# Linear attention and a mixture of experts in one kernel: VectorE's order in the middle of the attention

## The chip, the cores and the metric

One core of a Trainium2 chip runs the whole program. The metric is the time of one execution in microseconds on the device. TensorE does the matrix products (PE in the profile, PEld its weight loads), VectorE (DVE) and ScalarE (ACT) the elementwise work, GpSimd (POOL) a share of it and the indirect DMAs; SyncE (SP) issues the other DMAs.

## The reference, cut to what matters

```python
def phi(x):                                   # x: (8, 8, 576, 64) of q or k
    proj = einsum('bhsd,df->bhsf', x, w_phi)  # 128 features
    proj = proj - max(abs(proj), axis=-1)
    return concat([exp(proj), exp(-proj)])
kv  = einsum('bhsf,bhsd->bhfd', phi(k), v)
z   = sum(phi(k), axis=2)
num = einsum('bhsf,bhfd->bhsd', phi(q), kv)
den = einsum('bhsf,bhf->bhs', phi(q), z) + 1e-06
x   = num / den                               # as 4608 rows of 512
```

Then, over the 4608 rows: rows with `x @ w_skip > 0` go to the expert with the largest of 8 gate logits, `y = gate * (relu(x @ w1[e]) @ w2[e])`, and `x + y` is their output; the other rows stay as they are.

## The kernel before

The attention is cut into 16 units of k and 16 of q: a batch and four heads each, with `u.hq` 0 or 1 for the half of the heads. A unit has five items `i`: 0 is the tail of 64 tokens per head, 1 to 4 are blocks of 512 columns. The k stream runs six steps ahead of the q stream, and a step `t` does one stage of one item of each: transpose (`st_t`, lag 0), projection and subtraction of the largest magnitude (`st_proj`, lag 1), exponentials (`st_exp_k`, `st_exp_q`, lag 3; q is first transposed on TensorE), use (lag 4: `st_use_k` sums kv in bank K, `st_use_q` makes numerator, gate logits and denominator in a bank O), and for a finished k unit the sum z over partitions (`st_z`, lag 5) and the augmented matrix `kva` (`st_aug`, lag 6), which the numerators of that unit's q read.

PSUM has two buffers for projections (P), one for q's transposes (U), one for kv (K) and two for everything else (O): numerators, z sums, augmentation, ranks, indices and counts. Each use holds its buffer until the engine that reads it is done.

On VectorE a step has: transposes of raw blocks (`xT`, L331; tails `xTt`, L329), a reduce (`m`, L361) and a subtract (`u`, L364) over a projection of up to 1024 columns, and for each numerator a norm (`norm`, L467): add to the denominator (`den`, L471), reciprocal (`rec`, L475), two products (`xm` L482, `lgm` L483). When both halves of a batch are done, `post` picks each row's expert in a chain of small instructions (`L`, `mx`, `d`, `key`, `km`, `oh`, `OH`, then `ss`, `gt` and a reciprocal for the gate), and later `rank` (TensorE, then `rm`, `rki`, `rkp`, `RKH`, `st`, `Stot`, `rm4`; the one-hots `OP` are made on GpSimd), `index` (TensorE, then `acc4`) and `rest` (rows to the output) follow. Work that is put off stands in the list `later` with a due step; CFG["post"] is (4, 7, 7) for these three. For batch 5 (`EB`) the list also gets two `pick`s and `pick_third`, which choose the first experts' tokens so that their gathers can start early.

Order: `tc.manual_schedule` keeps the named engines in the order in which the program is written; engines that it does not name are ordered by the framework's planner at build time. Step 0 to 7 are one hand-written list (`RAMP`). From step 8 to 77 two steps are written as a pair, in the order of the list `PAIR`: `L` runs what is due, `T` transposes, `q` and `k` exponentials, `P` projections, `Z` and `A` z and augmentation, `U` use, `D` loads of v. TensorE and ScalarE are in program order up to step 78; SyncE and VectorE only up to step 17, and from 18 on they are ordered by the planner:

```python
man.enter_context(tc.manual_schedule(engines={PE, Activation}))     # closed at t == 79
ramp.enter_context(tc.manual_schedule(engines={SP, DVE}))           # closed at t == 18
PAIR = [('L', 0), ('T', 0), ('T', 1), ('q', 0), ('k', 0), ('P', 0), ('P', 1), ('Z', 0), ('L', 1),
        ('q', 1), ('A', 0), ('k', 1), ('U', 0), ('U', 1), ('D', 0), ('D', 1)]
```

After the attention the expert stage runs (the second half of the file); the change does not touch it. It needs the attention's memory, the picks and the first weights.

Of the kernel before, what the change touches and what calls it, by code (L numbers as in the profile page):

```python
# [24 lines left out]
def kernel(  # L25
# [230 lines left out]
    with actx:  # L256
# [77 lines left out]
        def st_proj():  # L334
# [11 lines left out]
            for u, i in todo:  # L346
# [11 lines left out]
                nj += m  # L358
            pv = p.rearrange("p h (j f) -> p j h f", f=NF)[:, 0:nj]
# [7 lines left out]
            for u, i, a, b in spans:  # L367
                u.u[i] = uu[:, a:b, :]

# [97 lines left out]
        def norm(o, xdst, ldst, shape):  # L467

            den = small.tile([P, 4], F32, tag="den", name="den")
            rec = small.tile([P, 4], F32, tag="rec", name="rec")  # L470
            nc.vector.tensor_scalar(  # L471
                out=den.rearrange("p (t o) -> p t o", o=1), in0=o[:, :, NA1:NAUG],
                scalar1=1e-6, scalar2=None, op0=ALU.add,
            )
            nc.vector.reciprocal(out=rec, in_=den)  # L475
            rv = rec.rearrange("p (t o) -> p t o", o=1)
            a, c = shape

            def sh(x):
                return x.rearrange("p (a c) d -> p a c d", a=a)  # L480

            nc.vector.tensor_tensor(out=xdst, in0=sh(o[:, :, 0:D]), in1=sh(rv.broadcast_to([P, 4, D])), op=ALU.mult)  # L482
            nc.vector.tensor_tensor(  # L483
                out=ldst, in0=sh(o[:, :, D:NA1]), in1=sh(rv.broadcast_to([P, 4, NA1 - D])), op=ALU.mult)

        def st_use_q(u, i):
# [5 lines left out]
            if i == 0:  # L492
# [11 lines left out]
                if u.hq == 0:  # L504
# [6 lines left out]
                     lgt[:, 0, u.hq * 4:(u.hq + 1) * 4, :].rearrange("p (a h) e -> p a h e", a=2), (2, 2))  # L511
# [13 lines left out]
            if u.hq == 0 and i == 1:  # L525
# [5 lines left out]
            norm(ov, xm[u.hq][:, 2 * th:2 * th + 2, 0:4 * D].rearrange(  # L531
                "p a (h r d) -> p a r h d", h=2, d=D)[:, :, pr],
                 lgm[:, 2 * th:2 * th + 2, h0:h0 + 2, :], (2, 2))
            if i == 4:
                c = slice(0, 4 * D)
                if u.hq == 0:
                    def store_half(b=u.b, xm=xm):
                        nc.sync.dma_start(out=rowm[b][:, :, c], in_=xm[0])
                        if b % 2 == 1:
                            nc.sync.dma_start(out=rowt[b // 2][:, c], in_=xt_of[b // 2][0][0][:, 0])  # L540
                    later.append((now[0] + 2, store_half))
                else:
                    post(u.b)

# [3 lines left out]
        def post(b):  # L548
# [25 lines left out]
            for xx, lg, o, n in reversed(parts):  # L574
                nc.vector.tensor_reduce(
                    out=L[:, o:o + n, :], in_=lg.rearrange("p t h e -> p t e h"), axis=AX.X, op=ALU.add,
                )
            nc.vector.tensor_reduce(out=mx[:, 0:nt], in_=L[:, 0:nt, 0:E], axis=AX.X, op=ALU.max)
            nc.vector.tensor_tensor(out=d[:, 0:nt], in0=L[:, 0:nt, 0:E], in1=bc(mx[:, 0:nt], nt, E), op=ALU.subtract)
            nc.vector.scalar_tensor_tensor(  # L580
                out=key[:, 0:nt], in0=d[:, 0:nt], scalar=0.0,
                in1=desc.rearrange("p (o e) -> p o e", o=1).broadcast_to([P, nt, E]),
                op0=ALU.is_equal, op1=ALU.mult,
            )
            nc.vector.tensor_reduce(out=km[:, 0:nt], in_=key[:, 0:nt], axis=AX.X, op=ALU.max)
            nc.vector.tensor_tensor(out=oh[:, 0:nt], in0=key[:, 0:nt], in1=bc(km[:, 0:nt], nt, E), op=ALU.is_equal)
            nc.vector.scalar_tensor_tensor(
                out=OH[:, T, :], in0=L[:, 0:nt, E:E + 1].broadcast_to([P, nt, E]), scalar=0.0, in1=oh[:, 0:nt],
                op0=ALU.is_gt, op1=ALU.mult,
            )  # L590

            def gate():
                nc.scalar.activation(out=ex[:, 0:nt], in_=d[:, 0:nt], func=AF.Exp)
                nc.vector.tensor_reduce(out=ss[:, 0:nt], in_=ex[:, 0:nt], axis=AX.X, op=ALU.add)
                nc.vector.tensor_scalar(out=gt[:, 0:nt], in0=ss[:, 0:nt], scalar1=1e-9, scalar2=None, op0=ALU.add)
                for xx, lg, o, n in parts:
                    nc.scalar.activation(
                        out=xx[:, :, 4 * D + 1:4 * D + 2], in_=sid[:, t0 + o:t0 + o + n].rearrange("p (t o) -> p t o", o=1), func=AF.Copy)
                    nc.vector.reciprocal(out=xx[:, :, 4 * D:4 * D + 1], in_=gt[:, o:o + n].rearrange("p (t o) -> p t o", o=1))

# [6 lines left out]
            if last:  # L607
                gate()
                store_rows()
            else:  # L610
                later.append((now[0] + 2, gate))
                later.append((now[0] + 4, store_rows))
# [4 lines left out]
            def rank():  # L617

# [13 lines left out]

                if last:
                    count()
                rm = sm("rm", [5, E])
                rki = sm("rki", [5], I32)
                rkp = sm("rkp", [5], I32)
                nc.vector.tensor_tensor(out=rm[:, 0:nt], in0=r.rearrange("p (t e) -> p t e", e=E), in1=OH[:, T, :], op=ALU.mult)
                with nc.allow_low_precision(reason="sums of integers below 2**24 written as integers"):
                    nc.vector.tensor_reduce(out=rki[:, 0:nt], in_=rm[:, 0:nt], axis=AX.X, op=ALU.add)  # L640
                nc.vector.tensor_scalar(out=rkp[:, 0:nt], in0=rki[:, 0:nt], scalar1=127, scalar2=None, op0=ALU.bitwise_and)
                for c in range(2):
                    for t in range(nt):
                        (nc.vector if last else nc.gpsimd).tensor_scalar(  # L644
                            out=OP[:, t0 + t, c, :], in0=iota_p, scalar1=rkp[:, t:t + 1],
                            scalar2=wcol[:, NT:NT + 1] if c else wcol[:, t0 + t:t0 + t + 1], op0=ALU.is_equal, op1=ALU.mult)
                nc.vector.tensor_scalar(out=RKH[:, T], in0=rki[:, 0:nt], scalar1=7, scalar2=None, op0=ALU.arith_shift_right)
                if not last:
                    count()
                if b > EB:  # L650
                    return
                for s in range(S):
                    nc.vector.scalar_tensor_tensor(
                        out=rm4[:, 0:nt, :, s], in0=bc(RKH[:, T], nt, E), scalar=float(s), in1=OH[:, T, :],
                        op0=ALU.is_equal, op1=ALU.mult,
                    )
# [121 lines left out]
        for t in range(n + OFF + LA):  # L778
            if t == 18:
                ramp.close()  # L780
# [537 lines left out]
```

## Time and profile before

| | us |
|---|---|
| median of 3 runs | 603.95 |
| lowest, highest | 603.88, 605.79 |
| profiled execution | 603.57 |
| its span, first to last instruction | 601.6 |

In the profile a row has a time or a total in microseconds, the line of the kernel (L361), the engine, the operation, and `out<-in` by the program's tile names. In brackets or behind `<-` stands what released an engine that had been idle. A matmul's end is modelled, a wait is counted from that end, and a weight load's wait is listed apart. Where rows of the timeline are merged, the count stands at the end (x64).

### The profile page before, as it was taken

The numbers are of one execution on the slowest core, as the hardware profiler recorded it, in microseconds if no ns is written. First come the engines' busy times: TensorE is split into PE (matmuls) and PEld (weight loads), VectorE is DVE, ScalarE is ACT, GpSimd is POOL, SyncE is SP. The second block draws the span as 40 slices with busy tenths as digits, with TensorE's granted clock in tenths as the row PEclk, the third lists the DMA queues.
The fourth block names the chain that finished last, engine by engine and source line by source line (L and its number), as shares of the span: only waits on it lengthen the run. The fifth ranks groups of instructions, "written<-read, shape, count | busy, mean of one in ns | idle before, by whom it ended". The sixth has DMA issues, their size and how long they took to land. (4 is left out here: it accounts for less than half of the span.)

```text
span 601.6 us, 18718 instructions
## 1 busy us (share of the span) xinstructions
PE 557.7 (93%) x7486; PEld 466.8 (78%) x7486; DVE 498.9 (83%) x1085; ACT 328.9 (55%) x649; POOL 375.6 (62%) x399
## 2 busy tenths in 40 slices
PE   5799899999999999999799799899999998999993
PEld 3577678778877778777667799798999887988892
DVE  5888998999989999899897759767789987867841
ACT  4466465666656655565444554354758666556720
POOL 6645486596675866848664645994668683638031
PEclk9999999999999999999899899899999999999998
DMA  8987998998668756531235297598787678777500
GB/s 146 160 143 141 181 184 177 208 186 194 139 147 194 150 135 155 122 95 46 87 115 177 75 325 260 156 310 286 216 275 241 231 269 299 255 225 255 191 20 30
DMA packets 250297, 108.33 MB, mean 180 GB/s; under 512 B 192481, under 2 KB 235617, under 8 KB 250208
## 3 DMA queue, kind: packets, MB, share of 16 engines
q1 hardware_dynamic: 244640, 97.45, 62.0%
q0 software_dynamic: 3200, 9.45, 4.3%
q8 instruction: 60, 0.98, 0.7%
q10 hardware_dynamic: 2368, 0.22, 0.3%
q14 instruction: 29, 0.24, 0.1%
HBM read 83.86 MB, written 24.02 MB: 179 GB/s over the span
## 5 line engine op out<-in xcount | busy, mean ns | idle before, releaser
L387 POOL TENSOR_TENSOR z<-ek 128x512 f32<-128x512 f32 x64 | 81.1, 1274 | 79.7 <-ACT ek L380 61.5
L200 POOL TENSOR_TENSOR w<-wraw_c,w 128x256 fp32r<-128x256 f32 x108 | 99.0, 950 | 48.3 <-ACT w L195 48.2
L195 ACT ACTIVATE w<-wraw_c 128x1024 fp32r<-128x1024 f32 x96 | 98.0, 1051 | 7.6 <-DMA wraw_c<-in_moe_w_dram 5.9
L200 DVE TENSOR_TENSOR w<-wraw_c,w 128x1024 fp32r<-128x1024 f32 x69 | 90.6, 1327 | 9.3 <-ACT w L195 7.8
L361 DVE TENSOR_REDUCE m<-ps_P 128x8 f32<-128x1024 f32 (+3 forms) x86 | 88.6, 1030 | 3.7 <-PE ps_P L354 3.7
L364 DVE TENSOR_TENSOR u<-ps_P,m 128x1024 f32<-128x1024 f32 (+3 forms) x86 | 88.7, 1032 | 3.1
L520 PEld LDWEIGHTS ps_O<-kva,eq 128*64 128x64 f32 x2048 | 74.4, 137 | 16.0 <-DVE cs L710 4.4
L354 PE MATMUL ps_P<-wsrc,xT 64*64 64x128 f32 x2048 | 74.5, 280 | 11.1 <-DVE xT L331 6.4
L406 ACT ACTIVATE eq<-ps_U 128x512 f32<-128x512 f32 x64 | 38.1, 596 | 83.1 <-PE ps_U L400 82.1
L520 PE MATMUL ps_O<-kva,eq 128*64 128x74 f32 x2048 | 77.3, 229 | 6.3 <-DVE cs L710 3.7
L354 PEld LDWEIGHTS ps_P<-wsrc,xT 64*64 64x64 f32 x2048 | 58.5, 136 | 22.8 <-issue 10.4
L422 PE MATMUL ps_K<-ek,v 128*64 128x256 f32 x512 | 68.4, 388 | 0.0
L903 POOL DMA_INDIRECT out_dram<-o,si x22 | 32.5, 1477 | 57.1 <-DVE si L902 50.6
L970 PE MATMUL ps_O<-w,hh 128*128 128x512 f32 x160 | 63.9, 399 | 0.7 <-DVE o L917 0.7
L644 POOL TENSOR_SCALAR OP<-iota_p,rkp,wcol 128x128 bf16<-128x128 f32 x62 | 48.5, 797 | 13.4 <-DVE rec L475 7.2
L400 PE MATMUL ps_U<-ident,u 128*128 128x128 f32 x288 | 49.2, 289 | 0.4 <-DVE den L471 0.3
L331 DVE STREAM_TRANSPOSE xT<-raw 128x512 f32<-128x512 f32 x64 | 43.5, 694 | 6.7 <-PE ps_P L354 3.4
L974 PE MATMUL ps_O<-w,hh 128*128 128x512 f32 x120 | 47.0, 391 | 0.1
L379 ACT ACTIVATE ek<-u 128x512 f32<-128x512 f32 x64 | 41.0, 640 | 11.1 <-DMA wgs<-in_moe_w_gate_dram 6.1
L975 PE MATMUL ps_O<-w,hlo 128*128 128x512 f32 x120 | 46.8, 390 | 0.0
L422 PEld LDWEIGHTS ps_K<-ek,v 128*64 128x64 f32 x512 | 32.9, 137 | 16.0 <-issue 6.2
L393 POOL TENSOR_TENSOR z<-z,ekt 64x512 f32<-64x512 f32 x32 | 40.8, 1274 | 5.1 <-DMA xg<-xrows,idg 2.8
(254 smaller groups left out, 1202.7 us busy)
## 6 DMA issues: line engine op xcount, KB each, us to landing
wraw_c<-in_moe_w_dram SPq DMA_DIRECT2D x96, 512.0 KB, 5.1
raw<-in_q_dram SPq DMA_DIRECT2D x64, 144.0 KB, 3.5
raw<-in_k_dram SPq DMA_DIRECT2D x60, 144.0 KB, 3.1
v<-in_v_dram SPq DMA_DIRECT2D x64, 128.0 KB, 2.6
out_dram<-xm SPq DMA_DIRECT2D x16, 512.0 KB
xrows<-xm SPq DMA_DIRECT2D x8, 516.0 KB, 3.9
xrows<-xm SPq DMA_DIRECT2D x8, 512.0 KB, 4.7
vt<-in_v_dram SPq DMA_DIRECT2D x32, 32.0 KB, 4.3
```

Source lines behind the costliest of these rows:

```text
L195: nc.scalar.activation(out=hi, in_=raw, func=AF.Copy)
L200: eng.tensor_tensor(out=lo[:, r], in0=raw[:, r], in1=hi[:, r].bitcast(F32), op=ALU.subtract)
L354: nc.tensor.matmul(p[s * 64:s * 64 + 64, hd, (nj + j) * NF:(nj + j + 1) * NF], xT[r, g * P + s * 64:g * P + s * 64 + 64], wsrc[r], start=T ...
L361: nc.vector.tensor_reduce(out=m.rearrange("p (j h) -> p j h", h=2), in_=pv, axis=AX.X, op=ALU.max, apply_absolute_value=True)
L364: nc.vector.tensor_tensor(out=uu[:, 0:2 * nj, :].rearrange("p (j h) f -> p j h f", h=2), in0=pv, in1=m.rearrange("p (j h o) -> p j h o", h ...
L387: zeng.tensor_tensor(out=z, in0=e[:, 0:2, :], in1=e[:, 2:4, :], op=ALU.add)
L400: nc.tensor.transpose(t[:, tt * P:(tt + 1) * P], uu[:, tt, :], ident)
L422: nc.tensor.matmul(o[hd * 64:hd * 64 + 64, :], u.v[:, 2 * hd + pr, g * D:(g + 1) * D], u.e[i][:, 2 * j + hd, :], start=(g == 0), stop=False,)
L520: nc.tensor.matmul(ov[s * 64:s * 64 + 64, 2 * j + hd, :], e[:, half, j, hd, s * 64:s * 64 + 64], kva[:, half, 2 * pr + hd, :], start=(half ...
L644: (nc.vector if last else nc.gpsimd).tensor_scalar(out=OP[:, t0 + t, c, :], in0=iota_p, scalar1=rkp[:, t:t + 1], scalar2=wcol[:, NT:NT + 1 ...
L970: nc.tensor.matmul(y[sub], hh[:, t], wh[:, fi, :], start=first, stop=False)
L974: nc.tensor.matmul(y[sub], hh[:, t], wl[:, fi, :], start=False, stop=False)
```

## The change

VectorE joins the engines in program order for steps 0 to 77, until t is 78; SyncE leaves program order at step 8 in place of 18. The order written out for VectorE is a new one. A pair now begins with the first transposes; then the norms of the pair before run together (`norms`: both additions, both reciprocals, then the products); then come the exponentials, both projections on TensorE, and only after them their reduces and subtracts (`st_diff`, `V`), the second transposes, both kv sums (`u`) and then both numerators (`n`). The chain of `post` becomes a generator; `hook` issues its next instruction, and stands after the norms, after each reduce and after each subtract, and inside a norm that has no partner. `drain` issues what is left of a batch's chain before its rank or index. The index comes 10 steps after `post` (8 for batch 5) in place of 7, the picks 9 and 11 in place of 8 and 10, the third at 13 in place of 12; what is due is looked at once in a pair.

```diff
-        PAIR = [('L', 0), ('T', 0), ('T', 1), ('q', 0), ('k', 0), ('P', 0), ('P', 1), ('Z', 0), ('L', 1), ('q', 1), ('A', 0), ('k', 1), ('U', 0), ('U', 1), ('D', 0), ('D', 1)]
+        PAIR = [('T', 0), ('N', 0), ('H', 0), ('q', 0), ('k', 0), ('P', 0), ('P', 1), ('L', 1), ('V', 0), ('V', 1), ('Z', 0), ('q', 1), ('A', 0), ('k', 1), ('T', 1), ('u', 0), ('u', 1), ('n', 0), ('n', 1), ('D', 0), ('D', 1)]
...
-        ramp.enter_context(tc.manual_schedule(engines={mybir.EngineType.SP, mybir.EngineType.DVE}))
+        dve = ExitStack()
+        dve.enter_context(tc.manual_schedule(engines={mybir.EngineType.DVE}))
+        ramp.enter_context(tc.manual_schedule(engines={mybir.EngineType.SP}))
...
-            if t == 18:
+            if t == 8:
                 ramp.close()
+                paired[0] = True
+            if t == 78:
+                drain()
+                norms()
+                drain()
+                paired[0] = False
+                dve.close()
...
+        def st_diff(got):
+            p, nj, spans = got
...
             nc.vector.tensor_reduce(
                 out=m.rearrange("p (j h) -> p j h", h=2), in_=pv, axis=AX.X, op=ALU.max, apply_absolute_value=True)
+            hook()
...
             for u, i, a, b in spans:
                 u.u[i] = uu[:, a:b, :]
+            hook()
...
+        def norms():
...
+            for o, xdst, ldst, den, rec in todo:
+                nc.vector.tensor_scalar(
+                    out=den.rearrange("p (t o) -> p t o", o=1), in0=o[:, :, NA1:NAUG],
+                    scalar1=1e-6, scalar2=None, op0=ALU.add,
+                )
+            if len(todo) == 1:
+                hook()
+            for o, xdst, ldst, den, rec in todo:
+                nc.vector.reciprocal(out=rec, in_=den)
+            if len(todo) == 1:
+                hook()
+            for o, xdst, ldst, den, rec in todo:
+                rv = rec.rearrange("p (t o) -> p t o", o=1)
+                nc.vector.tensor_tensor(
+                    out=xdst, in0=sh(o[:, :, 0:D]), in1=sh(rv.broadcast_to([P, 4, D])), op=ALU.mult)
+                nc.vector.tensor_tensor(
+                    out=ldst, in0=sh(o[:, :, D:NA1]), in1=sh(rv.broadcast_to([P, 4, NA1 - D])), op=ALU.mult)
...
+        def hook():
+            while chain:
+                try:
+                    next(chain[0][1])
+                    return
+                except StopIteration:
+                    chain.pop(0)
...
-                for n, f in zip(CFG["post"], (rank, index, rest)):
+                for n, f in ((4, rank), (8 if b == EB else 10, index), (7, rest)):
                     later.append((now[0] + n, f))
                 if b == EB:
                     for j in range(2):
-                        later.append((now[0] + CFG["post"][2] + 1 + 2 * j, lambda j=j: pick(j)))
-                    later.append((now[0] + CFG["post"][2] + 5, pick_third))
+                        later.append((now[0] + 9 + 2 * j, lambda j=j: pick(j)))
+                    later.append((now[0] + 13, pick_third))
```

Inside the chain the order is as before, with a `yield` after each instruction (after two of the four `rm4`, and after the exponential that the gate needs); the gate and the row store are its last pieces, where they used to be entries of `later` 2 and 4 steps on.

## Rows read from the trace of the kernel before

**Rows 1.** Page, part 1: busy time of each engine, its share, instructions

```profile
PE 557.7 (93%) x7486; PEld 466.8 (78%) x7486; DVE 498.9 (83%) x1085; ACT 328.9 (55%) x649; POOL 375.6 (62%) x399
```

**Rows 2.** Busy time in two stretches (us, times), clock, DMA share, GB/s

```profile
60.00:290.00 230.00, 219.08 (x4340) 176.36 (x4334) 219.00 (x532) 136.01 (x325) 160.45 (x148) 1.00 0.71 155
...
337.00:602.00 265.00, 246.94 (x1565) 221.84 (x1562) 193.66 (x336) 139.34 (x210) 153.30 (x168) 0.98 0.67 222
```

**Rows 3.** Waits of TensorE's matmuls, 60 to 290 us: total, times, longest

```profile
PE ps_O L499 <- ACT kva L461: 2.2, 3, 1.6
PE ps_P L354 <- DVE u L364: 2.1, 4, 1.0
PE ps_O L520 <- ACT kva L461: 2.0, 6, 0.3
PE ps_O L664 <- DVE den L471: 1.9, 3, 0.7
PE ps_O L664 <- POOL OP L644: 1.7, 3, 0.6
```

**Rows 4.** Waits of its weight loads there, those on another engine's work

```profile
PEld L664 <- POOL OP L644: 3.8, 9, 0.7
...
PEld ps_O L499 <- ACT kva L461: 3.5, 3, 2.0
PEld ps_O L520 <- ACT kva L461: 3.5, 6, 0.6
PEld ps_P L354 <- DVE u L364: 3.1, 4, 1.2
```

**Rows 5.** Waits of VectorE, 60 to 290 us

```profile
DVE xT L331 <- PE ps_P L354: 2.5, 7, 0.6
DVE den L471 <- PE ps_O L520: 2.1, 5, 0.4
DVE acc L670 <- PE ps_O L664: 0.9, 2, 0.5
```

**Rows 6.** Timeline of VectorE, 99 to 106 us: start, duration, instruction

```profile
99.53 1.19 DVE L361 TENSOR_REDUCE m<-ps_P 128x8 f32<-128x1024 f32 x1
100.82 1.22 DVE L364 TENSOR_TENSOR u<-ps_P,m 128x1024 f32<-128x1024 f32 x1
...
104.83 0.14 DVE L471 TENSOR_SCALAR den<-ps_O 128x4 f32<-128x4 f32 x1
105.00 0.18 DVE L475 RECIPROCAL rec<-den 128x4 f32<-128x4 f32 x1
105.22 0.42 DVE L482 TENSOR_TENSOR xm<-ps_O,rec 128x256 f32<-128x256 f32 x1
105.56 0.18 DVE L483 TENSOR_TENSOR lgm<-ps_O,rec 128x36 f32<-128x36 f32 x1
105.66 0.15 DVE L471 TENSOR_SCALAR den<-ps_O 128x4 f32<-128x4 f32 x1
```

**Rows 7.** Groups of VectorE, 60 to 290 us: busy, mean ns, idle before

```profile
L361 DVE TENSOR_REDUCE m<-ps_P 128x8 f32<-128x1024 f32 x36 | 43.3, 1203 | 0.0
...
L361 DVE TENSOR_REDUCE m<-ps_P 128x6 f32<-128x768 f32 x24 | 22.5, 936 | 0.0
...
L471 DVE TENSOR_SCALAR den<-ps_O 128x4 f32<-128x4 f32 x52 | 7.8, 149 | 2.1 <-PE ps_O L520 2.1
```

**Rows 8.** Timeline of all engines: two projections on TensorE, merged

```profile
136.06 1.98 PE L354 MATMUL ps_P<-wsrc,xT 64*64 64x128 f32 x64
```

**Rows 9.** Timeline of all engines about the first pick

```profile
292.58 1.98 PE L520 MATMUL ps_O<-kva,eq 128*64 128x74 f32 x32 [3.12 <-DVE cs L710]
...
293.44 1.21 POOL L213 DMA_INDIRECT xg<-xrows,idg  x1 [1.13 <-DVE idg L222]
...
298.69 1.27 POOL L393 TENSOR_TENSOR z<-z,ekt 64x512 f32<-64x512 f32 x1 [2.79 <-DMA xg<-xrows,idg]
```

**Rows 10.** Waits of VectorE, 24 to 60 us: the one on a load

```profile
DVE xTt L329 <- DMA raw<-in_q_dram: 1.7, 1, 1.7
```

More of the change, by code (lines that the diff above doesn't have):

```diff
@@ L465, in st_aug, with sh @@
             kva_of[u.g] = kva
[L467 to L484, printed above, removed]
+        def sh(x):
+            return x.rearrange("p (a c) d -> p a c d", a=2)
@@ new lines, in norms @@
+        def norms():
+            todo = []
+            for o, xdst, ldst, then in undone:
+                den = small.tile([P, 4], F32, tag="den", name="den")
+                rec = small.tile([P, 4], F32, tag="rec", name="rec")
+                todo.append((o, xdst, ldst, den, rec))
+            for o, xdst, ldst, den, rec in todo:
[15 more added lines that the diff above has]
+                    out=ldst, in0=sh(o[:, :, D:NA1]), in1=sh(rv.broadcast_to([P, 4, NA1 - D])), op=ALU.mult)
+            then = [d[3] for d in undone if d[3]]
+            undone.clear()
+            for f in then:
+                f()
@@ new lines, in norm, with drain @@
+        def norm(o, xdst, ldst, then=None):
+            undone.append((o, xdst, ldst, then))
+            if not paired[0]:
+                norms()
+        undone, chain, paired = [], [], [False]
+        def hook():
+            while chain:
+                try:
+                    next(chain[0][1])
+                    return
+                except StopIteration:
+                    chain.pop(0)
+        def drain(b=None):
+            while [c for c in chain if b in (None, c[0])]:
+                hook()
@@ L486, in st_use_q, with run_later @@
+        def run_later(b, g, front=False):
+            chain.insert(0 if front else len(chain), (b, g))
+            if not paired[0]:
+                drain()
         def st_use_q(u, i):
@@ L609, in post @@
                 store_rows()
-            else:
-                later.append((now[0] + 2, gate))
-                later.append((now[0] + 4, store_rows))
+            run_later(b, choose())
             S = 4
@@ L641, in rank @@
[L641 to L656, printed above, removed]
+                def turned():
+                    if last:
+                        count()
+                    rm = sm("rm", [5, E])
+                    rki = sm("rki", [5], I32)
+                    rkp = sm("rkp", [5], I32)
+                    nc.vector.tensor_tensor(
+                        out=rm[:, 0:nt], in0=r.rearrange("p (t e) -> p t e", e=E), in1=OH[:, T, :], op=ALU.mult)
+                    yield
+                    with nc.allow_low_precision(reason="sums of integers below 2**24 written as integers"):
+                        nc.vector.tensor_reduce(out=rki[:, 0:nt], in_=rm[:, 0:nt], axis=AX.X, op=ALU.add)
+                    yield
+                    nc.vector.tensor_scalar(out=rkp[:, 0:nt], in0=rki[:, 0:nt], scalar1=127, scalar2=None, op0=ALU.bitwise_and)
+                    for c in range(2):
+                        for t in range(nt):
+                            (nc.vector if last else nc.gpsimd).tensor_scalar(
+                                out=OP[:, t0 + t, c, :], in0=iota_p, scalar1=rkp[:, t:t + 1],
+                                scalar2=wcol[:, NT:NT + 1] if c else wcol[:, t0 + t:t0 + t + 1], op0=ALU.is_equal, op1=ALU.mult)
+                    yield
+                    nc.vector.tensor_scalar(
+                        out=RKH[:, T], in0=rki[:, 0:nt], scalar1=7, scalar2=None, op0=ALU.arith_shift_right)
+                    yield
+                    if not last:
+                        count()
+                        yield
+                    if b > EB:
+                        return
+                    for s in range(S):
+                        nc.vector.scalar_tensor_tensor(
+                            out=rm4[:, 0:nt, :, s], in0=bc(RKH[:, T], nt, E), scalar=float(s), in1=OH[:, T, :],
+                            op0=ALU.is_equal, op1=ALU.mult,
+                        )
+                        if s % 2 == 1:
+                            yield
@@ L660, in index @@
                     return
+                drain(b)
                 ix = bank("O")[:, 0:nsh]
@@ L790 @@
                 if c == "L":
+                    now[0] = t + (1 if first else 0)
                     for w, f in [x for x in later if x[0] <= now[0]]:
```

114 lines of the change are left out of this document (68 added, 46 removed).

## The prediction

> **What bounds the kernel now.** I read four views in this order. The busy times [rows 1] put TensorE at 93% of the span and VectorE at 83%. That is a mean over unlike stages, so the stretches come next [rows 2]: from 60 to 290 us, the middle of the attention, TensorE is busy 219.08 of 230 us and VectorE 219.00, both at 95%, with the clock at 1.00. From 337 us on the experts run and VectorE is at 73%. So the change lies in a stage where two engines look full at once, and the reader has to ask which of them waits for the other.
>
> The waits answer that. In 60 to 290 us TensorE's matmuls waited for other engines 9.9 us in 19 places (2.2, 2.1, 2.0, 1.9 and 1.7) [rows 3]; its weight loads waited for the same releasers 13.9 us in the four largest groups [rows 4]. VectorE in turn waited for TensorE only 5.5 us in its three largest groups [rows 5]. So neither has slack: TensorE follows its fixed order with few holes, and VectorE has hardly any idle time. But "busy" on VectorE hides something that the timeline shows [rows 6]. A reduce at 99.53 lasts 1.19, and the subtract that reads its result starts at 100.82, 0.10 after the reduce's end. The small product at 105.56 lasts 0.18, and the next norm's addition, which does not need it, starts at 105.66, 0.08 before that end. An instruction behind the one it reads costs about 0.18 us more than one that doesn't. One norm is a chain of such: addition at 104.83, reciprocal at 105.00, products at 105.22 and 105.56, next instruction at 105.66, so 0.83 us.
>
> **The bound in numbers, for ten steps.** The window holds 60 steps (36 + 24 reduces, [rows 7]), so ten steps take 230 / 6 = 38.3 us. TensorE without waits: by its matmuls 9.9 us could go, by its weight loads 13.9. I take 12.7, near the upper end: a matmul's end is modelled, and I estimate from the two views that it covers some 0.15 us of each of the 19 waits, so 9.9 + 2.8. That is 2.1 us of each ten steps (bounds 1.65 to 2.3), and TensorE alone needs 36.2. VectorE: 230 - 5.5 = 224.5 us of work with its bubbles, 37.4 per ten steps.
>
> **Part 1: two q norms interleaved.** Written as two additions, two reciprocals, then the products, no norm instruction stands behind the one that it reads. An independent small instruction starts 0.10 after the one before (105.56 to 105.66); the first two steps of a norm, 0.17 and 0.22, come down to 0.10 each, so 0.19 a norm and 0.38 for two: 1.28 us in place of 1.66 [rows 6]. There are 52 norms in the window [rows 7]; with the skipped tails 22 pairs of two and 8 singles, so 22 x 0.38 = 8.4 us, and some 0.8 for the singles, whose gaps take a chain instruction. The norms also move: they run at the head of the next pair, behind the first transposes. They hold an O bank that much longer, but the next user of one (rank or index, z) comes on TensorE only after both projections, 1.98 us for 64 matmuls [rows 8]. VectorE now waits there in order for the last numerator; queued behind it are the next reduces, which wait for projections that TensorE issues still later, so that wait costs little. The price if that cover is gone is the 1.28 us of the norms in each pair.
>
> **Part 2: chain instructions between the large ones.** About 20 of them in ten steps fill gaps behind a reduce or subtract. Their own time stays. Now the planner puts a transpose or a chain instruction into many of the reduce-subtract gaps; afterwards the transposes are elsewhere and some 3 or 4 of 10 such gaps stay open. No row gives the new count, so I bound it: 0 to 20 x 0.18 = 3.6 us of loss in the window, and take 1.5, below the middle, since some stand open now as at 99.53 [rows 6].
>
> VectorE afterwards: 224.5 - 8.4 - 0.8 + 1.5 = 216.8 us, or 36.1 per ten steps (35.9 without new gaps; 37.4 to 38.0 if interleaving brings nothing).
>
> **Part 3: kv sums ahead of numerators, index later.** On TensorE nothing is added. The numerators now stand behind both kv sums. Waits for `kva` (2.2 + 2.0, [rows 3]) end: ScalarE's copies have the kv sums' time to finish. The index matmuls come at +10 steps in place of +7, so the 1.7 us behind GpSimd's one-hots go, and, with the norms at the head of the pair, the 1.9 us for an O bank. The 2.1 us in which a projection waited for a subtract go if VectorE is not late: both subtracts of a pair stand ahead of its second transposes. VectorE may be late by about one projection (half of 1.98 us, [rows 8]) plus the q transposes before TensorE stalls, since the first projection of a pair needs only transposes of the pair before.
>
> **Part 4: the picks.** The choice of the first experts' tokens moves from steps 77 and 79 to 79 and 81. Today the first costs TensorE 3.12 us: its count matmul holds an O bank until VectorE's `cs`, and a numerator starts only at 292.58 [rows 9]. At 79 TensorE's order is the planner's again. I bound the gain by 3.1 and, with the work moved into the tail, -1, and take 1.5.
>
> **Queues.** SP's order is free from step 8 rather than 18: no row shows what that does to loads; the nearest price is VectorE's one wait of 1.7 us for `raw` before 60 us [rows 10], so -1.7 to +1.7, taken as 0. Row stores and GpSimd's one-hots are issued when their chain instruction comes, a step or two later; nobody reads them before the index or the gathers. The experts' 265 us [rows 2] only start earlier.
>
> **The sum.** Seventy steps run in the new order: 7 x 2.1 = 14.8 us is all that TensorE can give there (11.5 to 16). VectorE needs 36.1 against TensorE's 36.2, and the pairs differ (of each five pairs two also hold z sums and augmentation on TensorE, and another is long on VectorE: two full projections to reduce and two norms), so some new waits will remain; I keep about a fifth, 2.8 us, for them: 12.0. With 1.5 for the picks 13.5. The profiled execution is 603.57 us, its span 601.6; the median of 603.95 is 0.4 above it. 603.57 - 13.5 gives **590 us**.
>
> **Rivals.**
> VectorE sets the pace (18%): open gaps and lateness add 1 us to each ten steps, 37.0. Against it stands the sum of part 2, for it how thin 36.1 against 36.2 is. 7 x 1.3 = 9, less the picks' uncertainty: 594 to 600.
> Interleaving brings nothing (7%): if every VectorE instruction had to wait for the pipe to empty, the work stays at 37.4, so 7 x 0.9 plus 1.5: about 596. Rows 6 speak against it, as an independent instruction starts before the end of the one before. [...]
> All waits go (8%): the pairs give 7 x 2.3 = 16, the picks 1.5 to 3.1: 584 to 586.
> Slower (10%): the picks' gathers in the tail. Today GpSimd is held by the first from 293.44 to 298.69, its next z addition waiting 2.79 us for the gather [rows 9]. Two steps later such a hold, 5.3 us, with some 2.2 for the second (an estimate, under half of the first), could stand in front of the last z additions, which gate the last `kva` and all numerators behind it: 7.5 us at the end of the attention. It decides only if the pairs give less than that: with 3 us from them, 603.6 - 3 + 7.5 = 608.
>
> **How the numbers follow.** The forecast, 586 to 594, has 57%. The range should leave out no more than two tenths: 583 to 600 leaves out the slower case, and what lies between 600 and 604; its lower end takes in the case in which all waits go. About 0.3% (1.8 us) is what a measurement of this kernel can tell from no change. Faster: 57 + 18 + 7 + 8 less 6 for ends that fall short, 84%. Same 6%, slower 10%.
>
> **What would show it.** Right: the norms' den, den, rec, rec without gaps in VectorE's timeline, two norms in about 1.28 us; ten steps in 36.2 to 36.8 us; no waits of L520 or L499 for `kva` nor of the index matmuls for GpSimd; no 3 us hole at the first pick; the experts' stretch as long as before. Wrong: TensorE's projections waiting for `u` or `xT` in every cycle (VectorE is the bound), many reduce-subtract gaps of 0.10 us, or a hole of several us in front of the last z sums. What would upset the whole is a stage after 300 us that does not follow the attention's end.

## The result, and the profile after

The changed kernel takes 595.49 us, the median of six runs (593.79 to 597.11), against 603.91 for the kernel before (six runs, 603.09 to 605.79): a ratio of 0.9857, interval 0.984 to 0.9874. The forecast was 590, its range 583 to 600. Of the 13.5 us forecast, 8.4 came. One of the ten executions of a run below (`rm4` first, numerators straight behind their kv sums) took 778.62 us at a granted clock of 0.66, and is left out of that run's median.

The profiled execution took 596.92 us, its span 594.9, 1.4 above the median. So the two profiles differ by 6.7 us, and that is what can be followed in them. The page of the changed kernel, busy time, to be held against [rows 1]:

```profile
PE 558.0 (94%) x7486; PEld 467.8 (79%) x7486; DVE 500.4 (84%) x1085; ACT 328.6 (55%) x649; POOL 374.2 (63%) x399
```

Two stretches of it, as in [rows 2] (the second begins 7 us earlier, as the attention ends earlier):

```profile
60.00:290.00 230.00, 224.69 (x4471) 181.51 (x4461) 226.28 (x544) 140.35 (x334) 161.45 (x149) 1.00 0.69 153
...
330.00:595.00 265.00, 247.58 (x1567) 221.99 (x1565) 194.10 (x338) 139.33 (x210) 153.23 (x168) 0.97 0.67 222
```

The instructions are the same in number; in 60 to 290 us TensorE gets through 4471 matmuls in place of 4340, and VectorE is busy 98% of it. The waits there, of TensorE's matmuls, of its weight loads and of VectorE, to be held against [rows 3 to 5]:

```profile
PE ps_O L732 <- DVE lgm L500: 2.9, 1, 2.9
PE ps_O L461 <- DVE acc L740: 1.1, 2, 0.6
PE ps_P L354 <- DVE xT L331: 0.9, 1, 0.9
...
PEld L732 <- POOL z L395: 3.0, 1, 3.0
PEld ps_P L354 <- DVE xT L331: 2.9, 9, 1.2
PEld ps_O L461 <- DVE acc L740: 2.3, 4, 0.8
...
DVE m L367 <- PE ps_P L354: 1.1, 4, 0.4
```

The waits for `kva`, for `u` and for GpSimd's one-hots are gone. What is left is one wait of 2.9 us in one place, batch 5's index at 283 us, and small ones for `xT` and `acc`.

Where the time went can be read from the reduces of VectorE's timeline, one for each step (counted from 0). In us, between the starts of reduces; the last numerator is taken at the start of its last matmul, 0.23 us before that one's end; the third column is an experiment told below.

| stretch | before | after | without z sums |
|---|---|---|---|
| start to reduce 8 | 24.1 | 25.0 | 23.6 |
| 8 to 28 | 77.9 | 75.7 | 72.9 |
| 28 to 68 | 154.9 | 150.5 | 150.0 |
| 68 to 78 | 47.7 | 46.3 | 41.2 |
| 78 to the last numerator | 31.8 | 32.2 | 33.2 |
| from there to the end | 265.3 | 265.3 | (other work) |

Seventy steps (8 to 78) gave 8.0 us in these profiles, the stretch behind them -0.4, the start -0.9. Forecast were 12.0 for the seventy steps and 1.5 for the choices of experts' tokens. The two can't be told apart by this table: the holes of TensorE at the first choice, 3.12 us before [rows 9] and 1.63 us after, both lie ahead of reduce 78. The experts' stage is as long as before, as forecast. In the profile of after, 28 to 32 us ran at a mean granted clock of 0.57 (0.50 from 28.5 to 31.5 us, 1.00 again from 32.0) behind a hole of TensorE at 26.3 us, 1.9 us by its weight loads' wait and 1.63 by its matmuls':

```profile
28.00:32.00 4.00, 3.78 (x52) 2.64 (x53) 2.90 (x5) 0.50 (x2) 3.58 (x3) 0.57 1.10 173
```

A later run with the same order up to there and the same hole (with `rm4` first, below) kept 1.00 and was 1.5 us earlier at reduce 14 (46.5 against 48.0). That is about what the profiled execution lies above its median; without it, I estimate from these two runs, the seventy steps gave some 9.5.

**The steady part.** Forty steps, reduce 28 to reduce 68: length, then busy time (times) of TensorE, its weight loads, VectorE, ScalarE, GpSimd. The kernel before, then after:

```profile
102.00:256.80 154.80, 149.41 (x2976) 120.65 (x2972) 146.57 (x361) 92.25 (x221) 109.34 (x100) 1.00 0.73 162
```

```profile
100.70:251.20 150.50, 149.16 (x2975) 120.61 (x2973) 148.01 (x362) 92.66 (x221) 108.74 (x101) 1.00 0.76 162
```

TensorE has the same work, 149.4 and 149.2 us. Of the 5.4 us in which it stood before, 1.3 are left: it is full, at 37.6 us for ten steps, not at the 36.2 that the forecast took for its floor. VectorE is busy 37.0 for ten steps. The forecast's 36.1 counted otherwise, the stretch less VectorE's waits for TensorE, so with the gaps between instructions; by that count it is 37.5 before (154.8 less 4.8 of waits) and 37.5 after (150.5 less 0.5).

### The profile page after: what moved, and what is told of

Same layout as the page of the kernel before. It is cut to its first block, busy times and chain, and to the rows that moved or that the text cites. A ratio compares the mean times of both kernels' runs of the same rounds, so it can differ in the third digit from the quotient of the medians.

```text
span 594.9 us, 18720 instructions
## 1 busy us (share of the span) xinstructions
PE 558.0 (94%) x7486; PEld 467.8 (79%) x7486; DVE 500.4 (84%) x1085; ACT 328.6 (55%) x649; POOL 374.2 (63%) x399
## 5 line engine op out<-in xcount | busy, mean ns | idle before, releaser
L200 POOL TENSOR_TENSOR w<-wraw_c,w 128x256 fp32r<-128x256 f32 x108 | 98.8, 948 | 47.0 <-ACT w L195 36.5
L371 DVE TENSOR_TENSOR u<-ps_P,m 128x1024 f32<-128x1024 f32 (+3 forms) x86 | 90.1, 1048 | 4.2
L565 PEld LDWEIGHTS ps_O<-kva,eq 128*64 128x64 f32 x2048 | 72.6, 138 | 6.1 <-issue 0.5
L565 PE MATMUL ps_O<-kva,eq 128*64 128x74 f32 x2048 | 74.3, 229 | 0.2
L430 PE MATMUL ps_K<-ek,v 128*64 128x256 f32 x512 | 66.9, 392 | 0.0
L408 PEld LDWEIGHTS ps_U<-ident,u 128*128 128x128 f32 x288 | 30.4, 142 | 15.0 <-issue 7.5
```

What stands on the lines that cost most here:

```text
L200: eng.tensor_tensor(out=lo[:, r], in0=raw[:, r], in1=hi[:, r].bitcast(F32), op=ALU.subtract)
L371: nc.vector.tensor_tensor(out=uu[:, 0:2 * nj, :].rearrange("p (j h) f -> p j h f", h=2), in0=pv, in1=m.rearrange("p (j h o) -> p j h o", h ...
L408: nc.tensor.transpose(t[:, tt * P:(tt + 1) * P], uu[:, tt, :], ident)
L430: nc.tensor.matmul(o[hd * 64:hd * 64 + 64, :], u.v[:, 2 * hd + pr, g * D:(g + 1) * D], u.e[i][:, 2 * j + hd, :], start=(g == 0), stop=False,)
L565: nc.tensor.matmul(ov[s * 64:s * 64 + 64, 2 * j + hd, :], e[:, half, j, hd, s * 64:s * 64 + 64], kva[:, half, 2 * pr + hd, :], start=(half ...
```

## The experiments

Two things were open. Which engine holds the changed kernel, TensorE at a higher floor than thought or VectorE with more work than thought? And which part of the change brings what? The first four runs undid one part each, or took one load away.

**Norms one after the other.**

```diff
 for o, xdst, ldst, den, rec in todo:
     nc.vector.tensor_scalar(out=den...)
-...
-for o, xdst, ldst, den, rec in todo:
     nc.vector.reciprocal(out=rec, in_=den)
-...
-for o, xdst, ldst, den, rec in todo:
     nc.vector.tensor_tensor(out=xdst, ...)
```

> The changed kernel (595.5 us) with one part undone: the two norms of a pair run one behind the other, each addition, reciprocal, product, product; all else stays, their place at the head of the pair too. Theory A, VectorE sets the pace of the pairs: two norms take 1.66 us again in place of 1.28, 26 pairs x 0.38 = 9.9 us of VectorE, and nearly all of it shows: 603 to 606. Rival B, TensorE sets the pace and VectorE has slack: 0 to 3 us more, 595 to 598.5.

Measured: 625.09 us (624.11 to 627.29), ratio 1.0373. Neither reason given foresaw that. The timeline shows three holes of TensorE, twenty steps apart, 6.4 us by its weight loads' waits and 6.2 by its matmuls'. The first of them, VectorE, GpSimd and TensorE of this kernel, start and duration:

```profile
91.12 0.32 DVE L710 SCALAR_TENSOR_TENSOR rm<-RKH,OH 128x32 bf16<-128x32 int32 x2
92.19 7.58 DVE L710 SCALAR_TENSOR_TENSOR rm<-RKH,OH 128x32 bf16<-128x32 int32 x2
...
85.98 6.24 POOL L697 TENSOR_SCALAR OP<-iota_p,rkp,wcol 128x128 bf16<-128x128 f32 x8 [3.67 <-DVE rkp L694]
92.18 2.51 POOL L395 TENSOR_TENSOR z<-ek 128x512 f32<-128x512 f32 x2
94.66 1.26 POOL L399 TENSOR_TENSOR z<-z 128x512 f32<-128x512 f32 x1
95.89 1.25 POOL L395 TENSOR_TENSOR z<-ek 128x512 f32<-128x512 f32 x1
97.11 1.25 POOL L401 TENSOR_TENSOR z<-z,ekt 64x512 f32<-64x512 f32 x1
98.33 1.25 POOL L399 TENSOR_TENSOR z<-z 128x512 f32<-128x512 f32 x1
...
102.34 0.92 PE L354 MATMUL ps_P<-wsrc,xT 64*64 64x128 f32 x12 [6.20 <-DVE xT L331]
```

The first two of the four small products `rm4` (two inputs in SBUF) run beside a one-hot `OP` in 0.32 us. The next two come at 92.19, as the one-hots end and six z additions that had queued up behind them begin, without a gap between them. They end at 99.77, just behind the sixth, and everything of VectorE stands behind them. In the changed kernel the same products meet the last one-hots (93.23 and 93.42, 0.31 and 0.22 us, the last ending at 93.64 while the one-hot runs to 93.81): it escapes by less than 0.2 us. So this run does not price the norms; it shows a trap beside them.

**No z additions.**

```diff
-z = zp.tile([P, 2, 2 * NF], F32, tag="z", name="z", bufs=5)
-zeng.tensor_tensor(out=z, in0=e[:, 0:2, :], in1=e[:, 2:4, :], op=ALU.add)
-u.z[i] = z
-...
+u.z[i] = zconst
```

> The changed kernel without GpSimd's z additions: a constant tile stands for z, so the denominators are left uncomputed in part. All other instructions stay. In the changed kernel 23 small instructions of VectorE before 280 us last 0.31 to 1.69 us in place of about 0.18, and most of them end 0.03 to 0.06 us behind a z addition; together some 9 us too long. Theory A, they are held by GpSimd's additions and VectorE sets the pace: all of them fall to 0.2 us or less and the time falls by 6 to 9 us, to 586.5 to 589.5. Rival B, the length is their own or lies beside waits: 0 to 2 us less, 593.5 to 595.5.

Measured: 628.6 us, but that says nothing: this run leaves out the denominators' sums, so that the experts are chosen by other numbers, and the experts' stage is 40 us longer. The attention can be compared. Its last numerator stands at 320.96 us against 329.58 after the change, 8.6 earlier. The table above shows where: 1.4 us before reduce 8, 2.7 in reduces 8 to 28 (some 1.5 of it the clock), 5.0 in 68 to 78, 1.0 lost behind, and only 0.5 in the forty steps between. So the lengths did fall, as theory A had it (`d` to 186 ns, `key` to 181), but in the steady part hardly any time with them. There VectorE is relieved by 4.4 us and TensorE is not faster:

```profile
96.60:246.60 150.00, 148.69 (x2974) 120.52 (x2972) 143.62 (x362) 92.61 (x221) 27.99 (x36) 1.00 0.77 164
```

So TensorE's floor is 37.5 us for ten steps, where the forecast had 36.2. VectorE without holds is busy 35.9, and needs some 36.5 by the forecast's count (150.0 less 3.8 of waits), where the forecast had 36.1.

**Second transposes ahead of the first reduce; and numerators straight behind their kv sums.**

```diff
-('V', 0), ('V', 1), ..., ('k', 1), ('T', 1), ('u', 0), ...
+('T', 1), ('V', 0), ('V', 1), ..., ('k', 1), ('u', 0), ...
```

> The changed kernel with the second transposes of a pair moved from behind both subtracts to ahead of the first reduce. Theory A: the first projection of the next pair needs these transposes, so they are late when VectorE is; the hole of 1.9 us at 26 us and the low clock behind it go (3 us by step 14), and the small holes in front of later projections; 591 to 594. Rival B: the hole at 26 us is made up by step 18 anyway, as before and after stand 0.3 us apart there, and the reduces start 0.65 us later: 595 to 597.

```diff
-('u', 0), ('u', 1), ('n', 0), ('n', 1)
+('u', 0), ('n', 0), ('u', 1), ('n', 1)
```

> The changed kernel with kv sums and numerators in the old order (sum, numerator, sum, numerator). TensorE's waits for kva come back: 4.2 us by its matmuls' rows, 7 by its weight loads', in 60 to 290 us of the kernel before. Theory A, VectorE sets the pace: they hide in part, 0 to 2.5 us more, 595 to 598. Rival B, TensorE sets it: 5 to 8 us more, 600 to 603.5.

Measured: 606.99 us (ratio 1.006, 1.0038 to 1.0083) and 619.86 (1.0282, 1.0255 to 1.0308). All four expectations missed. In both runs the trap is back: one hole of 6.0 us (by the weight loads) at 96 us in the first, with holds of 1.1 to 1.4 us later; three of 5.9 us in the second, where a product `rm4` lasts 7.5 us. The early hole at 26 us is gone in the first.

**The same with the trap taken away.** Four runs put `rm4` ahead of the one-hots, alone and with each of the three edits:

```diff
+RKH and the four products rm4
 rkp; one-hots OP on GpSimd
-RKH
 count()
-the four products rm4
```

> The changed kernel with the four products rm4 of each batch (two SBUF inputs each) put ahead of GpSimd's one-hots OP instead of behind them in VectorE's chain. In the changed kernel these products run beside OP in 0.2 to 0.3 us each and cost little, so both theories expect about its 595.5 us here. Train theory (a two-input VectorE instruction that comes while GpSimd works off its z additions is held by them; rm4 behind OP meets the additions that OP has backed up): 594 to 598, with no hold over 2.6 us (two z additions) on any rm4; single z additions may hold some. Rival (place theory: the three holes of 6 us in the runs before come from the place of the norms, transposes or numerators themselves): also 594 to 598. This run is the base for the next three.

> The norms written one after the other, as in the run of 625.1 us, with rm4 ahead of OP. Train theory: the three holes of 6.45 us are gone, so 625.1 - 3 x 6.4 = 606, between 603 and 609; what stays against the run with rm4 first alone, 8 to 12 us, is the price of the norms apart. Rival (place theory): the holes stay, 620 or more.

> The second transposes ahead of the first reduce, as in the run of 607.0 us, with rm4 ahead of OP. Train theory: the 6.0 us hole at 96 us and the later ones of one or two z additions are gone, and the early hole of 26 us too: 591 to 597. Rival (place theory): the transposes' place delays the first reduce and with it TensorE in every pair; 602 or more.

> Numerators right behind their kv sums, as in the run of 619.9 us, with rm4 ahead of OP. Train theory: the three holes of 5.94 us are gone: 619.9 - 17.8 = 602, between 598 and 604; what stays against the run with rm4 first alone is the price of the waits for kva (about 0.6 us in each of seven or eight cycles of ten steps, 4 to 5 us). Rival (place theory): the holes come from the numerators' place, 614 or more.

Measured, with the profiled execution's reduces 28 to 68 and its last numerator:

| run | median | ratio, interval | 28 to 68 | last numerator |
|---|---|---|---|---|
| rm4 first | 602.58 | 0.9964 (0.9937 to 0.9992) | 154.4 | 332.17 |
| and norms apart | 607.59 | 1.0041 (1.0013 to 1.0069) | 158.8 | 339.92 |
| and transposes first | 603.65 | 0.9985 (0.9959 to 1.0012) | 156.0 | 334.11 |
| and numerators straight behind | 603.84 | 0.9972 (0.9941 to 1.0002) | 155.0 | 334.06 |

The holes of 6 us are gone in all, as the train of additions foretold: 625.1 became 607.6, 619.9 became 603.8. But the base is not the 595 that both reasons expected: it was 598.6 in its profiled execution and spread to 605. With it the run with the transposes first missed its 591 to 597 (603.65 lies where the place theory had it, but without the hole), and the two prices expected against the base, 8 to 12 us for the norms and 4 to 5 for the waits for `kva`, came out smaller. Ahead of the one-hots the products meet single z additions instead. The group of `rm4` in 60 to 290 us and TensorE's waits for `xT` in this run (busy, mean ns; the mean was 236 after the change):

```profile
L703 DVE SCALAR_TENSOR_TENSOR rm<-RKH,OH 128x32 bf16<-128x32 int32 (+1 forms) x24 | 9.7, 466 | 0.0
...
PEld ps_P L354 <- DVE xT L331: 7.0, 17, 1.2
```

In the forty steps VectorE is busy 152.6 us in place of 148.0, and they last 154.4 in place of 150.5: 4.5 us more work made 3.9 us more time. So VectorE has hardly any slack: the changed kernel sits in the corner where both engines are full. Against this base, interleaving the norms is worth 5.0 us in the medians and 4.4 in the forty steps; at the last numerator it is 7.7, but the base's profiled execution lies 4 us under its median. The kv sums ahead of the numerators are worth 1.3 in the medians (the waits for `kva`, 1.9 us in six places, are back without them) and the transposes' place 1.1: the intervals overlap that of the base over most of their width, so neither can be told from nothing. Not tried was the new order with VectorE left to the planner, nor the old step for the index of the other batches; what these parts are worth stays open.

**The chain in one piece.**

```diff
 norms
-hook()
 V: reduce
-hook()
 subtract
-hook()
+if it is the pair's second: drain()
```

> The changed kernel with the chain instructions put in one piece behind the second subtract of each pair instead of singly behind reduces and subtracts. Theory (VectorE has about 0.6 us to spare in ten steps, 148.0 busy of 150.5 in forty, and some 20 chain instructions in ten steps lose their 0.18 us each): 7 x (3.6 - 0.6) = 21 at most, half of it if half of the instructions are independent of the one before: 604 to 616. Rival (TensorE sets the pace at 37.4 in ten steps and the chain's place is free): 593 to 598.

Measured: 639.77 us (639.23 to 641.04), ratio 1.0577, far above both. The instructions' 0.18 us are not what counts. One cycle of this kernel, TensorE, VectorE and ScalarE:

```profile
111.78 0.64 PE L446 MATMUL ps_O<-z,ones_f 128*32 128x256 f32 x8
...
116.16 0.77 PE L459 MATMUL ps_O<-aug,kvs 128*128 128x146 f32 x4 [3.15 <-DVE acc L736]
...
115.92 0.18 DVE L736 COPY acc<-ps_O 128x32 f32<-128x32 f32 x1
...
117.36 0.24 ACT L648 ACTIVATE ex<-d 128x40 f32<-128x40 f32 x1 [5.34 <-DVE d L632]
117.69 0.36 ACT L449 ACTIVATE zs<-ps_O 128x256 f32<-128x256 f32 x1
```

The copy `acc` frees an O bank for which TensorE waits 3.15 us, because it now stands behind two reduces and two subtracts. In the changed kernel it stands behind the first reduce, 1.1 us after that one's start (106.53 and 105.40) in place of 4.4 (115.92 and 111.54). ScalarE has `ex` in its order where the chain is written, waits 5.34 us for `d`, and the copy `zs` behind it, for which TensorE waits next, comes that much later. These waits are only part of the price. In 107.0 to 287.7 us, the forty steps here, TensorE's matmuls wait 18.4 us for `acc`, `zs` and `kva`; its work there takes 162.3 us at a mean granted clock of 0.92, in place of 149.2 at 1.00 after the change. So of the 30 us that these steps last longer, some 13 go with the lower clock that followed the holes (0.57 from 119 to 125 us).

**The late spots.** The last three runs mend places in which TensorE stands after the change. In the changed kernel, VectorE, GpSimd and TensorE about the last pair:

```profile
282.63 2.48 DVE L331 STREAM_TRANSPOSE xT<-raw 128x512 f32<-128x512 f32 x4
285.03 0.19 DVE L486 TENSOR_SCALAR den<-ps_O 128x4 f32<-128x4 f32 x2
286.74 3.58 DVE L798 TENSOR_TENSOR acc<-acc 128x16 f32<-128x16 f32 x1
...
282.87 3.73 POOL L395 TENSOR_TENSOR z<-ek 128x512 f32<-128x512 f32 x3
286.54 2.52 POOL L399 TENSOR_TENSOR z<-z 128x512 f32<-128x512 f32 x2
...
286.07 0.40 PE L732 MATMUL ps_O<-rm,OP 128*128 128x32 bf16 x10 [2.86 <-DVE lgm L500]
...
293.52 0.44 PE L354 MATMUL ps_P<-wsrc,xT 64*64 64x128 f32 x6 [1.63 <-DVE mx L775]
```

```diff
-(8 if b == EB else 10, index)
+(10, index)
-now[0] + 9 + 2 * j, pick(j)     now[0] + 13, pick_third
+now[0] + 11 + 2 * j, pick(j)    now[0] + 15, pick_third
```

> The changed kernel with batch 5's index matmuls ten steps behind their choice in place of eight, and the three choices of experts' tokens two steps later each. In the changed kernel TensorE stands 3.09 us from 282.98 (the index waits for an O bank whose norm stands behind four transposes) and 1.90 us from 291.62 (VectorE held 3.58 us in one small subtraction on acc by three z additions). Theory (from 282 us the index and the choices, not the pairs, are late last): both holes shrink by 3 to 5 us together, the last numerator comes at 325 to 327 in place of 329.58, and the time is 590.5 to 593.5. Rival (the tail is bound by VectorE's work there, and the choices moved into it stand in front of the last norms and z additions): 595 to 602.

```diff
+PAIR8 = PAIR with ('T', 1) ahead of ('V', 0), for t in (8, 10)
```

> The same with the second transposes ahead of the first reduce in the first two pairs only, where TensorE has a hole of 1.90 us from 26.32 in the changed kernel. Theory (that hole, and in some executions a lower clock behind it, is lost time, since TensorE sets the pace from then on): 1 to 3 us below the run before, 588 to 592. Rival (made up by the twentieth reduce in any case): as the run before within 0.7 us.

Measured: 594.69 us (593.42 to 595.8), ratio 0.9832 (0.9807 to 0.9856); with the early transposes 593.87 (592.3 to 594.52), ratio 0.9808 (0.9783 to 0.9833). The last numerator of the first stands at 325.80, 3.8 us earlier, a number that was expected, but 2.2 of it are there at reduce 68 (248.98 against 251.15), ahead of all that this edit moves. The edit gave 1.6, not 3 to 5, and the time is hardly shorter: the first expert's matmul then waits for its rows,

```profile
330.62 0.58 PE L1048 MATMUL ps_P<-x,w 128*128 128x256 f32 x1 [3.56 <-ACT x L925]
```

where the changed kernel waits 1.4 us. What was won in the last steps was lost behind the attention. The early transposes save 1.2 us from reduce 8 to reduce 68 (223.4 against 224.6), which were not made up by the twentieth reduce as the rival had it; in the medians the difference of 0.8 us lies within their spread.

```diff
 first two pairs: ('T', 1) ahead of ('V', 0)
 last pair: norms, then ('T', 1)
-a2 = a4[:, :, 2:4] - a4[:, :, 0:2];  a2 = a2 * po
+a2 = a4[:, :, 2:4] * po;  a2 = a2 - tp
```

> The changed kernel with three single spots mended, the index and the choices of experts' tokens left where they are: the second transposes ahead of the first reduce in the first two pairs; in the last pair the second transposes behind the norms that the index waits for; and the subtraction on acc that was held 3.58 us made dependent on the choice (the same value from the products by the choice), so that it can't be started ahead. Theory (TensorE sets the pace, so each of its holes in these spots is lost time: 1.9 us at 26.3, 3.1 at 283.0 of which the norms themselves need 1.4, 1.9 at 291.6): 1 + 1.6 + 1.9 us and up to 1.5 from the clock at 28 us, so the last numerator at 323.5 to 326 and 589 to 592 us. Rival (the last numerators wait for the z additions and the choices behind these holes anyway): the last numerator at 327 or later and 593 to 595 us.

Measured: 592.63 us (592.07 to 595.04), ratio 0.9814 (0.979 to 0.9838), between the two expectations: lowest median of all, its interval just below that of the changed kernel (0.984 to 0.9874), though it overlaps those of the two runs above. The index waits 1.0 us in place of 2.86, and the hole at 291 us is gone:

```profile
282.30 0.40 PE L732 MATMUL ps_O<-rm,OP 128*128 128x32 bf16 x10 [1.00 <-POOL z L395]
...
287.01 1.69 PE L354 MATMUL ps_P<-wsrc,xT 64*64 64x128 f32 x38
```

The last numerator stands at 326.1, between the two as well. Reduces 76 to 78 take 14.0 us in place of 16.7; from there to reduce 85 it is 23.9 in place of 22.8.

## Why the prediction was right, and where it was not

**The bound (the step that failed in size).** The forecast took 12.7 us of waits in 60 to 290 us, 2.1 for ten steps, and multiplied by seven. Its floor of 36.2 for TensorE lies below the 36.5 that the busy time of [rows 2] gives for a sixth of the window. Two of [rows 3] show in their last column why that was too much: of 2.2 us for `kva` 1.6 were one wait, of 2.1 for `u` 1.0. These two lie before 102 us and never come again. In the forty steps from 102.0 to 256.8 the matmuls of the kernel before waited 5.0 us in all, 1.25 for ten steps, and after the change there is one row, of new waits:

```profile
PE ps_O L520 <- ACT kva L461: 1.3, 4, 0.3
PE ps_O L664 <- DVE den L471: 1.3, 2, 0.7
PE ps_O L664 <- POOL OP L644: 1.1, 2, 0.6
PE ps_P L354 <- DVE u L364: 0.7, 2, 0.4
PE ps_O L499 <- ACT kva L461: 0.6, 2, 0.3
```

```profile
PE ps_O L461 <- DVE acc L740: 1.1, 2, 0.6
```

The stretch is 4.4 shorter: 5.0 gone, 1.1 new, and some 0.5 besides. So the matmuls' own waits were nearly the right count; the addition of 0.15 us for each wait, from the weight loads, brought another 2.8 in 230 us, where at most the 0.5 in forty steps came. The old waits were worth some 1.4 for ten steps, not 2.1, and with the new ones 1.1 came where 1.7 were forecast. The window was also not 60 steps of TensorE's work: it held 4340 matmuls, and forty steps hold 2976, so 58.3 steps, of which ten keep TensorE busy 37.6 us. That is the floor that came.

The fifth kept back for new waits (1.6 us in forty steps) was near the 1.1 that came, but it had been put there for VectorE's margin of 0.1 us against a floor that is higher than that. The sum was 12.0 for the pairs and the profile has 8.0. That the time still lies in the range is owed to its width, which took in a rival with another mechanism.

**Part 1, the norms: right.** The timeline of after shows two norms together, from 103.96 to the next instruction at 105.20, 1.24 us; forecast were 1.28 in place of 1.66 [rows 6]:

```profile
103.96 0.19 DVE L486 TENSOR_SCALAR den<-ps_O 128x4 f32<-128x4 f32 x2
104.12 0.25 DVE L493 RECIPROCAL rec<-den 128x4 f32<-128x4 f32 x2
104.33 0.42 DVE L498 TENSOR_TENSOR xm<-ps_O,rec 128x256 f32<-128x256 f32 x1
...
105.20 0.28 DVE L628 TENSOR_REDUCE L<-lgt 128x9 f32<-128x72 f32 x1
```

With the norms apart and the trap out of the way the two take 103.86 to 105.52, 1.66 us, and forty steps 4.4 us more than without that edit; the forecast's 9.2 in sixty steps would be 6.1 in forty. An instruction that needs nothing of the one before it does start before that one's end: the second `xm` at 104.77, where `lgm` lasts from 104.67 to 104.85. The rival by which every VectorE instruction waits for the one before it to be out of the pipe would have made this run as fast as the one with the norms interleaved; the two are 5.0 us apart (607.59 and 602.58). The traces show starts and ends of instructions; a pipe that has to be empty is shown by none.

**Part 2, the chain: the cost was of another kind.** The forecast looked for open gaps, and there are some (99.43 to 99.54 behind a reduce). What it did not see is that a small instruction sent off alone often meets an addition on GpSimd. Groups of VectorE in 60 to 290 us, of the kernel before and of after (busy, mean ns):

```profile
L579 DVE TENSOR_TENSOR d<-L,mx 128x32 f32<-128x32 f32 (+1 forms) x6 | 2.1, 355 | 0.2
L580 DVE SCALAR_TENSOR_TENSOR key<-d,desc 128x32 f32<-128x32 f32 (+1 forms) x6 | 1.4, 228 | 0.0
L585 DVE TENSOR_REDUCE km<-key 128x4 f32<-128x32 f32 (+1 forms) x6 | 1.0, 163 | 0.0
```

```profile
L634 DVE TENSOR_TENSOR d<-L,mx 128x32 f32<-128x32 f32 (+1 forms) x6 | 4.3, 717 | 0.0
L636 DVE SCALAR_TENSOR_TENSOR key<-d,desc 128x32 f32<-128x32 f32 (+1 forms) x6 | 3.8, 637 | 0.0
L798 DVE TENSOR_TENSOR acc<-acc 128x16 f32<-128x16 f32 x1 | 3.6, 3578 | 0.0
L642 DVE TENSOR_REDUCE km<-key 128x4 f32<-128x32 f32 (+1 forms) x6 | 1.1, 184 | 0.0
```

`d`, `key` and `OH` (181 to 439 ns), with two inputs in SBUF, grew two- or threefold. So did `gt` (153 to 464), which has one; the other chain instructions with one (`km`, `mx`, `ss`) stayed under 0.19 us in the mean, and `oh`, with two, fell from 364 to 185, as no addition ran beside it any more. Without z additions `d`, `key`, `OH` and `gt` take 186, 181, 186 and 160 ns. Over `d`, `key`, `gt`, `OH` and that one `acc` the holds add up to 12.7 us in the window (mean less the mean without z, times the count). Some 5.9 of them lie in the forty steps, and there they took back about what the norms' order saved: by the forecast's count VectorE needs 37.5 for ten steps as before, not 36.1. In time they cost little there, since without them only 0.5 us was gained; in the last pair they cost the hole at 291 us. And the chain's instructions release other engines, which the forecast did not weigh at all: in one piece they cost 44 us against the changed kernel, the lower clock included.

**Part 3 and 4.** The waits named went as told. The index's wait for an O bank did not go in the last pair, where four transposes stand ahead of the norm. What the choices gave can't be read off by itself; TensorE's hole of 3.12 us at the first one became 1.63, with the hold of 3.58 us in front of it, and the stretch behind reduce 78 is 0.4 longer.

**Queues and experts.** The experts' 265.3 us are unchanged. The 0 for SP's queue can't be told: reduce 8 starts at 23.6 to 25.7 us in runs whose order up to there is the same or nearly so.

**Rivals.** The time lies where "VectorE sets the pace" put it, and VectorE's 37.0 us busy, 37.5 with its gaps, are near what that rival asked for, but the mechanism is not shown to be the cause: with VectorE relieved by 4.4 us, forty steps gain 0.5. TensorE's floor of 37.5 is the nearer reason. "Slower", by the gathers in front of the last z additions, did not come: two gathers at 297.72 and 299.23 take 2.2 us together, and the z addition behind them starts at 300.20. "All waits go" came true for the old waits of the steady part, but they were worth about two thirds of what was taken.

## What to carry to other kernels

Before a wait is multiplied by the number of cycles, cut the window to whole cycles of the steady part and look at the longest wait beside the total: one wait of 1.6 us in a row of 2.2 is no rate. Work moved on one engine is priced by what it releases on the others and by what it meets there, not only by its gaps; where two engines are both full, as here, relief on the one gave 0.5 of 4.4 us and a load on it cost 3.9 of 4.5. When an experiment comes out far from every theory, look for one long instruction in the timeline before pricing the edit.

## What the runs showed of the hardware

VectorE instructions with two inputs in SBUF that came while GpSimd added two SBUF tiles lasted until an addition was over: eleven of `d`, `key` and `OH` in 60 to 290 us of the changed kernel ended 0.04 to 0.06 us behind one's end. So `d` at 110.37 lasted 0.84 us, to 111.21, beside an addition from 109.87 to 111.15, and 0.19 in the mean in the run without z additions.

```profile
109.87 1.28 POOL L395 TENSOR_TENSOR z<-ek 128x512 f32<-128x512 f32 x1
110.37 0.84 DVE L634 TENSOR_TENSOR d<-L,mx 128x40 f32<-128x40 f32 x1
```

`gt`, a small instruction with one SBUF input, was held as well: 0.38 to 0.68 us beside additions, 0.16 without; `mx` and `ss`, also with one, lasted 0.17 to 0.19 us beside them. The one-hots of GpSimd (one SBUF tile and scalars) did not visibly hold `rm4`, 0.21 to 0.31 us in the changed kernel; the sum `Stot`, also with two inputs, lasted 0.17 us beside them in three batches of the changed kernel and 0.34 in three. With additions back to back, a pair of products took 7.58 us, through six of them (norms apart), and `acc` stood through three, 3.58 us, while in the run with the transposes first two products got through after one each (1.14 and 1.35 us). What decides between these was not tried, nor was why the one-hots do not hold, nor why `gt` is held and `mx` is not. Behind the hole of 6.2 us that came of it, TensorE ran at a granted clock of 0.50 from 102 to 104 us in the run with the norms apart.
